# Slot softmax in single steps with its multiply on GpSimd, two-term folds for batch 0, and a new order of pieces

## The chip, the cores and the metric

The kernel runs on one core of one Trainium2 chip. The time is that of the device for one execution, in microseconds. TensorE is the matrix engine (PE in the profile, and PEld for its loads of weights), VectorE is DVE, ScalarE is ACT, GpSimd is POOL and SyncE is SP.

## The reference

Eight batches (B = 8) of eight heads (H = 8) with 576 positions (S) of 64 values (D) go through an attention over 32 memory slots, and the result goes through a feed-forward network with a maximum over three products.

```
a      = softmax over the 32 slots of phi            [8, 8, 576, 32]
k_m    = a^T k,   v_m = a^T v                        [8, 8, 32, 64]
attn   = softmax over the 32 slots of (q k_m^T / 8)  [8, 8, 576, 32]
x      = attn v_m, heads side by side                [4608, 512]
h      = max(x w1, x w2, x w3)                       [4608, 768]
out    = h w_out                                     [4608, 512], float32
```

## The kernel before

**Algebra.** The heads' outputs x are never built. For each batch v_m is multiplied into the weights first ("fold", piece D): since x = attn v_m, x w = attn (v_m w), and v_m w has 256 rows (8 heads of 32 slots), held as two groups of 128 (NG = 2). The maximum over three products is taken as max(x (w1 - w3), x (w2 - w3), 0) + x w3, so that the FFN has two products and a relu, and the x w3 part goes to the output as attn (v_m (w3 w_out)). The subtraction w1 - w3 and w2 - w3 is made in place in w_sb by w_diff (piece V, L182), in bfloat16, on VectorE. w3 w_out is made once, out of transposes of w3 (piece W) and products with w_out (piece O).

**Pieces.** The kernel is a list of pieces, written out by hand or by a planner as one string of tokens (L487 to L508). A token has a letter, often a number, the batch after "@", and "!" where the copy out of PSUM goes to the other engine (VectorE or ScalarE) than EVAC names at L133. Each engine does its instructions in the order of the tokens, and waits, in this order, for what it needs. So a token fixes the place of its instructions in every queue that they use: TensorE, VectorE, ScalarE, GpSimd, and SyncE's queue of output stores.

- H, L, Y: loads, all issued by GpSimd (H, batch 0's k and v in halves; L0 phi, L1 k, L2 v, L3 q of a later batch; Y0 to Y2 w1, w2, w3, Y3 w_out). Only batch 0's phi is loaded by SyncE. k, v, q and the weights are changed to bfloat16 on the way. phi and q have two buffers, k and v one pair for even and one for odd batches, so a load waits until the batch two earlier has been used.
- E: exp of phi (ScalarE). B: a^T [k, v, 1] (TensorE, L212). N: division by the sums (VectorE). K: transpose of the result (TensorE) and its copy, kvt. Q: 32 x 32 transposes of q (VectorE, L269), one half each.
- S: scores (TensorE, L291), and two exps (ScalarE, L300), one for each group g.
- X (att_mul): the slot softmax of group g, five VectorE instructions one after the other: transpose of 32 x 32 blocks into t (L313), sum over slots sm (L315), reciprocal (L316), multiply t by it (L317), transpose back into attn (L323).
- D: fold, eight matmuls on 64 x 32 tiles of the array (L341), and the copy into wp, or for D3 into wp3, the fold of w3 w_out.
- F (ffn1): hidden slice ft = n // 2; the even n is the relu of the w1 product (h1), the odd n the maximum of the w2 product with it (VectorE, L380), into hT. Each has four matmuls of 288 columns (L367).
- T (ffn2): 128 rows of output, six matmuls with w_out (L398) and two with wp3 (L407, or L416 for the tile that two batches share), a copy, a store. The last tile is made in halves (L439, L447).
- I: the identity matrix (GpSimd). Z: matmuls on zeros that keep TensorE going while the first loads arrive.

All products share four PSUM buffers of two banks each (acc_pool), taken in turn: a product waits until the one four before it has been copied out.

**What sets the order at the start.** Batch 0 has its fold in four parts, D0, D1, D2 and D4, with the columns of FIRST (L172): 0 to 512, 512 to 768, 768 to 1024 and 1024 to 1536 of w1 and w2 side by side. Before the fold of a part its w_diff has to be done, which needs w3 (Y2) and w1 (Y0) or w2 (Y1).

Of the kernel before, what the change touches and what calls it, by code (L numbers as in the profile page):

```python
# [15 lines left out]
def kernel(  # L16
# [159 lines left out]

    def w_diff(n):

        c, end = FIRST[n]
        while c < end:  # L180
            e = min(end, (c // DF + 1) * DF)
            nc.vector.tensor_tensor(  # L182
                out=w12[:, :, c:e],
                in0=w12[:, :, c:e],
                in1=w_sb[:, :, 2, c % DF : c % DF + e - c],
                op=ALU.subtract,
            )
# [85 lines left out]
    def att_score(b):  # L276
# [22 lines left out]
        for a in range(NG):  # L299
# [4 lines left out]
                scale=0.125,  # L304
            )

    def att_mul(b, g):
        s = st[b]
        e2 = s["e2"][:, g]
        t = work.tile([P, S // HP, R, 2], BF16, name="t", tag=f"t{g}")  # L310
        tf = t.rearrange("p n r e -> p (n r e)").bitcast(FP32)
        tv = t.rearrange("p n r e -> p n e r")
        nc.vector.transpose(out=tf, in_=e2.bitcast(FP32))  # L313
        sm = work.tile([P, S // HP, 2], FP32, name="sm", tag=f"sm{g}")
        nc.vector.tensor_reduce(out=sm, in_=tv, op=ALU.add, axis=mybir.AxisListType.X)  # L315
        nc.vector.reciprocal(out=sm, in_=sm)  # L316
        nc.vector.tensor_tensor(  # L317
            out=t,
            in0=t,
            in1=sm.unsqueeze(2).to_broadcast([P, S // HP, R, 2]),  # L320
            op=ALU.mult,
        )
        nc.vector.transpose(  # L323
            out=attns[b // 2][:, g, (b % 2) * S : (b % 2 + 1) * S].bitcast(FP32), in_=tf
        )
# [3 lines left out]
    def fold(b, n, swap):  # L329
# [5 lines left out]
        elif b not in wps:  # L335
            wps[b] = work.tile([P, NG, 2 * DF], BF16, name="wp")
        ps = acc_pool.tile([P, NG, BANK], FP32, name="wps", tag="acc")
        for j in range(NP):
            for a in range(NG):
                r = slice(HP * a, HP * (a + 1))  # L340
                nc.tensor.matmul(  # L341
                    ps[M * j : M * (j + 1), a, 0 : hi - lo],
                    lhsT=s["kvt"][r, 0, M * j : M * (j + 1)],
                    rhs=(w3o if n == 3 else w12)[r, j, lo:hi],
                    start=True,
                    stop=True,
                    tile_position=(HP * a, M * j),
                )
# [190 lines left out]
```

## Time and profile before

| | |
|---|---|
| median of 13 runs | 169.68 us (169.18 to 170.18) |
| the profiled execution's own time | 169.5 us |
| its span, first to last instruction | 167.7 us |
| granted TensorE clock | 0.995 |
| TensorE matmuls busy | 157.4 us, 94% |
| VectorE busy | 110.4 us, 66% |
| ScalarE busy | 98.9 us, 59% |
| GpSimd busy | 28.4 us, 17% |
| VectorE L317, the multiply | 16 times, 758 ns |
| VectorE L315, the sum over slots | 16 times, 753 ns |
| TensorE L128, on zeros | 16.4 us busy |

The page gives an engine's busy time over the whole span. The chain of waits goes back from the last instruction: at each step to what released it, or to the instruction before it on its engine; a line of it holds the start, the length, and what ran, with the number of instructions merged. The timeline gives an engine's instructions in order of time, with the idle time before each and what ended it in brackets. A load's own instruction on GpSimd takes about 0.75 us; the transfer goes on after it, and the page's last part gives the time from issue to landing. Matmuls are pipelined and the profile models their ends, so their steps from start to start are read rather than their lengths.

### The profile page before, as it was taken

How to read it: one execution, taken by the hardware profiler on the slowest of the kernel's cores; microseconds unless marked ns; L12 is line 12 of the kernel's file. 1: busy time of each engine (PE TensorE's matmuls, PEld its weight loads, DVE VectorE, ACT ScalarE, POOL GpSimd, SP SyncE). 2: the span in 40 equal slices, each digit the busy share in tenths (PEclk: the TensorE clock that was granted, in tenths of full speed). 3: DMA queues.
4: the chain of work that ended last, by engine and by line, in shares of the span. 5: the costliest groups of instructions: out<-in, count | busy, mean ns of one | idle time of the engine just before them, and what ended most of it. 6: DMA issues, size and time to landing. Idle time of an engine off the chain costs nothing.

```text
span 167.7 us, 4603 instructions
## 1 busy us (share of the span) xinstructions
PE 157.4 (94%) x1971; PEld 86.9 (52%) x1992; DVE 110.4 (66%) x198; ACT 98.9 (59%) x145; POOL 28.4 (17%) x43
## 2 busy tenths in 40 slices
PE   7998799999979999999998999999999999999991
PEld 2444533674337535755674355766533577644450
DVE  5406876895787959789778999997599456610000
ACT  4100514943888278898675998738678877222420
POOL 7952100040261313304010500000000000000000
PEclk9999999999999999999999999999999999999998
DMA  5999999999999999999999999961113310033433
GB/s 155 156 204 212 205 210 247 240 207 340 269 280 264 207 232 329 244 233 207 238 287 248 281 260 258 235 116 65 68 63 129 125 63 6 0 125 149 164 125 127
DMA packets 21973, 31.76 MB, mean 189 GB/s; under 512 B 1216, under 2 KB 16576, under 8 KB 21952
## 3 DMA queue, kind: packets, MB, share of 16 engines
q0 software_dynamic: 16080, 21.43, 66.5%
q1 hardware_dynamic: 5728, 9.90, 16.6%
q8 instruction: 15, 0.25, 0.5%
q10 hardware_dynamic: 144, 0.13, 0.2%
q14 instruction: 6, 0.05, 0.1%
HBM read 39.32 MB, written 9.44 MB: 291 GB/s over the span
## 4 chain that ended last, share of the span: by engine, by line
PE 57%; DMA 20%; DVE 15%; issue 4%; POOL 2%; ACT 1%; POOLq 0%; ACTq 0%
PE acc L367 23%; DMA kvo<-in_v_dram 20%; PE po L398 19%; PE po L407 5%; DVE t L317 4%; DVE sm L315 4%; PE wps L341 3%; DVE attn L323 2%; PE kvp L212 2%; DVE t L313 2%; PE sc L291 2%; DVE sm L316 1%; PE po L416 1%; POOL kvo L94 1%; PE po L439 1%
## 5 line engine op out<-in xcount | busy, mean ns | idle before, releaser
L367 PE MATMUL acc<-attn,wp 128*128 128x288 bf16 x384 | 50.8, 286 | 1.6 <-DVE attn L323 1.4
L398 PE MATMUL po<-wo_sb,hT 128*128 128x512 bf16 x192 | 50.2, 380 | 0.9
L367 PEld LDWEIGHTS <-wp 128*128 128x128 bf16 x384 | 36.5, 98 | 14.6 <-issue 2.0
L380 DVE TENSOR_TENSOR hT<-acc,h 128x576 bf16<-128x576 f32 x48 | 34.5, 752 | 13.0 <-PE acc L367 6.3
L141 ACT COPY ot<-po 128x512 f32<-128x512 f32 x35 | 20.7, 591 | 28.9 <-PE po L407 24.4
L139 ACT ACTIVATE h<-acc 128x576 bf16<-128x576 f32 x46 | 28.5, 655 | 8.6 <-PE acc L367 7.5
L398 PEld LDWEIGHTS <-hT 128*128 128x128 bf16 x210 | 19.1, 98 | 24.2 <-issue 4.6
L141 ACT CAST wp<-wps 128x1024 bf16<-128x1024 f32 (+1 forms) x31 | 29.7, 1015 | 0.9 <-PE wps L341 0.9
L300 ACT ACTIVATE e<-sc 128x576 bf16<-128x576 f32 x16 | 9.6, 653 | 15.2 <-PE sc L291 15.2
L407 PE MATMUL po<-wp,attn 128*128 128x512 bf16 x62 | 18.4, 379 | 0.0
L128 PE MATMUL po<-warm 128*128 128x512 bf16 x62 | 16.4, 422 | 1.4 <-DVE warm L120 1.2
L317 DVE TENSOR_TENSOR t<-t,sm 128x576 bf16<-128x576 bf16 x16 | 12.1, 758 | 0.5
L315 DVE TENSOR_REDUCE sm<-t 128x18 f32<-128x576 bf16 x16 | 12.0, 753 | 0.6
L269 DVE STREAM_TRANSPOSE qT<-qq 128x576 f32<-128x576 f32 x16 | 12.0, 762 | 0.5 <-DMA qq<-in_q_dram 0.5
L128 PEld LDWEIGHTS <-warm 128*128 128x128 bf16 x64 | 6.5, 106 | 9.6 <-issue 3.2
L199 ACT ACTIVATE e<-ph 128x1152 bf16<-128x1152 f32 (+1 forms) x9 | 9.5, 1061 | 2.6 <-DMA ph<-in_phi_dram 2.6
L456 DVE COPY ot<-po 128x256 f32<-128x256 f32 x1 | 0.4, 425 | 15.8 <-PE po L447 15.8
L90 POOL DMA_DIRECT2D ph<-in_phi_dram x7 | 5.3, 760 | 31.7 <-ACT e L199 27.3
L313 DVE STREAM_TRANSPOSE t<-e 128x288 f32<-128x288 f32 x16 | 7.3, 455 | 4.0 <-ACT e L300 4.0
L407 PEld LDWEIGHTS <-attn 128*128 128x128 bf16 x62 | 6.1, 98 | 7.3
L94 POOL DMA_DIRECT2D kvo<-in_k_dram x9 | 6.7, 744 | 15.6 <-PE wps L341 13.1
L102 POOL DMA_DIRECT2D qq<-in_q_dram x8 | 6.0, 750 | 16.3 <-DVE qT L269 15.7
(46 smaller groups left out, 110.9 us busy)
## 6 DMA issues: line engine op xcount, KB each, us to landing
out_dram<-ot SPq DMA_DIRECT2D x35, 256.0 KB, 2.4
qq<-in_q_dram POOLq DMA_DIRECT2D x8, 576.0 KB, 18.9
ph<-in_phi_dram POOLq DMA_DIRECT2D x7, 576.0 KB, 20.1
kvo<-in_k_dram POOLq DMA_DIRECT2D x7, 576.0 KB, 16.2
kvo<-in_v_dram POOLq DMA_DIRECT2D x7, 576.0 KB, 19.1
w_sb<-in_moe_w_dram POOLq DMA_DIRECT2D x3, 768.0 KB, 19.3
wo_sb<-in_moe_w_out_dram POOLq DMA_DIRECT2D x1, 768.0 KB, 16.4
ph<-in_phi_dram SPq DMA_DIRECT2D x2, 288.0 KB, 3.4
```

The costliest lines, as they stand in the source:

```text
L128: nc.tensor.matmul(po[:, 0:BANK], lhsT=warm[:, 0:P], rhs=warm, start=True, stop=True)
L139: nc.scalar.activation(out=out_, in_=in_, func=AF.Relu)
L141: nc.scalar.copy(out=out_, in_=in_)
L269: nc.vector.transpose(out=s["qT"][:, j].rearrange("p j c r e -> p (j c r e)").bitcast(FP32), in_=loaded[b]["q"][:, j].rearrange("p j c d - ...
L300: nc.scalar.activation(out=e2[:, a].rearrange("p (t r c) -> p t r c", t=2, c=NC), in_=sc[a][:, :, 0:SH].rearrange("p t (c r) -> p t r c", ...
L313: nc.vector.transpose(out=tf, in_=e2.bitcast(FP32))
L315: nc.vector.tensor_reduce(out=sm, in_=tv, op=ALU.add, axis=mybir.AxisListType.X)
L317: nc.vector.tensor_tensor(out=t, in0=t, in1=sm.unsqueeze(2).to_broadcast([P, S // HP, R, 2]), op=ALU.mult,)
L367: nc.tensor.matmul(acc[:, h, 0:SH], lhsT=wps[b][:, g, w * DF + ft * P : w * DF + (ft + 1) * P], rhs=attn[:, g, c0 : c0 + SH], start=(g == ...
L380: nc.vector.tensor_tensor(out=hT[:, ft, (b % 2) * S : (b % 2 + 1) * S].rearrange("p (h n) -> p h n", h=2), in0=a, in1=s["h1", ft], op=ALU.max,
L398: nc.tensor.matmul(po, lhsT=hT[:, fc, c0 : c0 + P], rhs=wo_sb[:, fc, :], start=(n == 0), stop=False,)
L407: nc.tensor.matmul(po, lhsT=attn[:, g, c0 : c0 + P], rhs=wp3s[b][:, g, :], start=False, stop=(g == NG - 1),)
```

## The change

The slot softmax of X is split into five tokens, so that its steps can be placed one by one: a (transpose), s (sum), c (reciprocal), m (multiply), X (transpose back). The multiply m is issued on GpSimd in place of VectorE. In batch 0 the folds D0, D1, D2 and D4 no longer read w1 - w3 and w2 - w3: they read w1 or w2 as loaded with kvt, and add a second product of minus kvt (the new tile kvtn, copied by ScalarE with a factor of -1 when kvt is copied) with w3. The subtractions (V) then serve batches 1 to 7 alone, come after batch 0's folds, and are cut into three equal parts of 512 columns. The list of tokens is new as a whole. The attn tile of a pair of batches is made by whichever batch asks first.

```diff
--- before.py
+++ after.py
@@ -176,7 +176,7 @@
 
     def w_diff(n):
 
-        c, end = FIRST[n]
+        c, end = n * BANK, (n + 1) * BANK
         while c < end:
             e = min(end, (c // DF + 1) * DF)
             nc.vector.tensor_tensor(
@@ -186,9 +186,6 @@
                 op=ALU.subtract,
             )
             c = e
-
-
-
 
     st = {}
 
@@ -258,6 +255,9 @@
         if part != 1:
             s["kvt"] = work.tile([P, 3, P], BF16, name="kvt")
         evacuate("K", 0, swap, s["kvt"][:, ns], ps[:, ns])
+        if b == 0 and part != 0:
+            s["kvtn"] = const.tile([P, P], BF16, name="kvtn")
+            nc.scalar.mul(out=s["kvtn"], in_=ps[:, 0], mul=-1.0)
 
     def att_q(b, n):
 
@@ -278,7 +278,7 @@
         s = st[b]
         kvt, qT = s["kvt"], s["qT"]
         e2 = s["e2"] = work.tile([P, NG, S], BF16, name="e2")
-        if b % 2 == 0:
+        if b // 2 not in attns:
             attns[b // 2] = work.tile([P, NG, 2 * S], BF16, name="attn")
         sc = [
             acc_pool.tile([P, 2, BANK], FP32, name="sc", tag="acc") for _ in range(NG)
@@ -304,24 +304,42 @@
                 scale=0.125,
             )
 
+    def att_t(b, g):
+        s = st[b]
+        t = s["t", g] = work.tile([P, S // HP, R, 2], BF16, name="t", tag=f"t{g}")
+        nc.vector.transpose(
+            out=t.rearrange("p n r e -> p (n r e)").bitcast(FP32),
+            in_=s["e2"][:, g].bitcast(FP32),
+        )
+
+    def att_sum(b, g):
+        s = st[b]
+        sm = s["sm", g] = work.tile([P, S // HP, 2], FP32, name="sm", tag=f"sm{g}")
+        nc.vector.tensor_reduce(
+            out=sm,
+            in_=s["t", g].rearrange("p n r e -> p n e r"),
+            op=ALU.add,
+            axis=mybir.AxisListType.X,
+        )
+
+    def att_rec(b, g):
+        s = st[b]
+        nc.vector.reciprocal(out=s["sm", g], in_=s["sm", g])
+
     def att_mul(b, g):
         s = st[b]
-        e2 = s["e2"][:, g]
-        t = work.tile([P, S // HP, R, 2], BF16, name="t", tag=f"t{g}")
-        tf = t.rearrange("p n r e -> p (n r e)").bitcast(FP32)
-        tv = t.rearrange("p n r e -> p n e r")
-        nc.vector.transpose(out=tf, in_=e2.bitcast(FP32))
-        sm = work.tile([P, S // HP, 2], FP32, name="sm", tag=f"sm{g}")
-        nc.vector.tensor_reduce(out=sm, in_=tv, op=ALU.add, axis=mybir.AxisListType.X)
-        nc.vector.reciprocal(out=sm, in_=sm)
-        nc.vector.tensor_tensor(
+        t = s["t", g]
+        nc.gpsimd.tensor_tensor(
             out=t,
             in0=t,
-            in1=sm.unsqueeze(2).to_broadcast([P, S // HP, R, 2]),
+            in1=s["sm", g].unsqueeze(2).to_broadcast([P, S // HP, R, 2]),
             op=ALU.mult,
         )
+
+    def att_back(b, g):
         nc.vector.transpose(
-            out=attns[b // 2][:, g, (b % 2) * S : (b % 2 + 1) * S].bitcast(FP32), in_=tf
+            out=attns[b // 2][:, g, (b % 2) * S : (b % 2 + 1) * S].bitcast(FP32),
+            in_=st[b]["t", g].rearrange("p n r e -> p (n r e)").bitcast(FP32),
         )
 
     wps, wp3s = {}, {}
@@ -335,17 +353,21 @@
         elif b not in wps:
             wps[b] = work.tile([P, NG, 2 * DF], BF16, name="wp")
         ps = acc_pool.tile([P, NG, BANK], FP32, name="wps", tag="acc")
-        for j in range(NP):
-            for a in range(NG):
-                r = slice(HP * a, HP * (a + 1))
-                nc.tensor.matmul(
-                    ps[M * j : M * (j + 1), a, 0 : hi - lo],
-                    lhsT=s["kvt"][r, 0, M * j : M * (j + 1)],
-                    rhs=(w3o if n == 3 else w12)[r, j, lo:hi],
-                    start=True,
-                    stop=True,
-                    tile_position=(HP * a, M * j),
-                )
+        terms = [(s["kvt"][:, 0], w3o[:, :, lo:hi] if n == 3 else w12[:, :, lo:hi])]
+        if b == 0 and n != 3:
+            terms.append((s["kvtn"], w_sb[:, :, 2, lo % DF : lo % DF + hi - lo]))
+        for i, (lhs, rhs) in enumerate(terms):
+            for j in range(NP):
+                for a in range(NG):
+                    r = slice(HP * a, HP * (a + 1))
+                    nc.tensor.matmul(
+                        ps[M * j : M * (j + 1), a, 0 : hi - lo],
+                        lhsT=lhs[r, M * j : M * (j + 1)],
+                        rhs=rhs[r, j, :],
+                        start=(i == 0),
+                        stop=(i == len(terms) - 1),
+                        tile_position=(HP * a, M * j),
+                    )
         evacuate(
             "D", n, swap, wp3s[b] if n == 3 else wps[b][:, :, lo:hi], ps[:, :, 0 : hi - lo]
         )
@@ -473,7 +495,11 @@
             "K": lambda: att_kv_t(b, swap, i),
             "Q": lambda: att_q(b, i),
             "S": lambda: att_score(b),
-            "X": lambda: att_mul(b, i),
+            "a": lambda: att_t(b, i),
+            "s": lambda: att_sum(b, i),
+            "c": lambda: att_rec(b, i),
+            "m": lambda: att_mul(b, i),
+            "X": lambda: att_back(b, i),
             "D": lambda: fold(b, i, swap),
             "F": lambda: ffn1(b, i, swap),
             "T": lambda: ffn2(b, i, swap),
@@ -485,24 +511,28 @@
 
 
     for w in """
-        H3@0 H0@0 H2@0 I@0 H1@0 E@0 Z38@0 B@0 L3@0 N@0 Y2@0 Z3@0 K@0 Q0@0 Q1@0 Z7@0 S@0 X0@0
-        Z6@0 W2@0! W0@0 Y3@0 Y0@0 W1@0 Z10@0 O1@0 O3@0 X1@0 V1@0 V0@0 O2@0 O0@0 D1@0 Y1@0 L0@1
-        D0@0! D3@0 V2@0 F10@0 V4@0 L1@1 F8@0 L3@1 F6@0 D2@0 F0@0! F2@0 D4@0 F3@0 F4@0 E@1 L2@1
-        F1@0 F11@0 F7@0 L0@2 F9@0 F5@0 B0@1 T3@0 N0@1 L0@3 K0@1! Q0@1 T2@0! B1@1 Q1@1 S@1 E@2
-        L2@2 L1@2 L0@4 N1@1 K1@1 T1@0 X0@1 D0@1 D1@1! L3@2 T0@0! D3@1 L1@3 L2@3 L3@3 D2@1 X1@1
-        F6@1! F0@1 F1@1 F2@1 F4@1 F7@1 F5@1 E@3 F8@1 F3@1 F10@1 F11@1 F9@1 B@2 N@2 L0@5 Q0@2
-        T1@1 L1@4 E@4 K@2 T4@1! Q1@2 S@2 T2@1! D0@2 D1@2! T0@1! X0@2 D3@2 B@3 X1@2 D2@2 T3@1
-        N@3 F6@2 Q0@3 Q1@3 F0@2 F1@2 F8@2 F7@2 L2@4 F4@2 K@3 L3@4 L1@5 F10@2 F9@2 S@3 L2@5
-        F11@2 F2@2 E@5 F5@2 F3@2 D2@3 D1@3! X0@3 X1@3 T2@2! D0@3 B@4 N@4 D3@3 T0@2! Q1@4 T3@2
-        F4@3 F6@3 K@4 F8@3 Q0@4 F9@3 F2@3 F0@3 F7@3 F1@3 F10@3 L3@5 F11@3 D0@4 B@5 D1@4! D2@4
-        T1@2 L0@6 L1@6 N@5 Q0@5 K@5 L2@6 F3@3 F5@3 S@4 E@6 Q1@5 T4@3! L0@7 X0@4 S@5 T1@3 D1@5!
-        X1@4 D0@5 T2@3! X1@5 L3@7 D2@5 B@6 D3@4 F10@4 N@6 E@7 X0@5 T3@3 F8@4 F6@4 F9@4 F11@4
-        F2@4 F4@5 L3@6 Q1@7 F7@4 F6@5 L1@7 F5@5 F8@5 Q1@6 F0@4 F7@5 F4@4 K@6 L2@7 Q0@7 F5@4
-        Q0@6 T0@3! F3@4 F1@4 F0@5 F1@5 F2@5 F10@5 F3@5 D2@6 B@7 D3@5 D3@6 T3@4 N@7 K@7 F9@5
-        F11@5 S@6 T4@5! S@7 T3@5 D1@6! D1@7! X0@6 D3@7 T0@5! X0@7 T2@4! D0@7 D0@6 D2@7 T1@4
-        T1@5 X1@7 X1@6 F6@6 F8@6 F10@6 F2@7 F3@7 F0@6 F7@6 F9@6 F2@6 F3@6 F1@6 F4@7 F11@6 F10@7
-        F4@6 F11@7 F6@7 F0@7 F5@7 F8@7 F9@7 F1@7 T0@4! F7@7 F5@6 T0@7! T1@7 T1@6 T0@6! T2@7!
-        T2@5! T2@6! T3@6 T4@7! T3@7
+        H3@0 I@0 E@0 H2@0 H1@0 H0@0 Z38@0 B@0 N@0 Z3@0 K@0 L3@0 Q1@0 Y2@0 Y3@0 Y0@0 Q0@0 Z7@0
+        S@0 a0@0 s0@0 Z6@0 W0@0 W2@0 W1@0 Z10@0 O2@0 a1@0 s1@0 c1@0 Y1@0 c0@0 m0@0 X0@0 O0@0
+        m1@0 O1@0 X1@0 D0@0 D1@0! O3@0 F4@0 V0@0 L0@1 L1@1 L3@1 F0@0 F2@0! F10@0! D2@0 D4@0
+        F8@0 V2@0 F3@0 F1@0 L2@1 F6@0 E@1 F11@0 F9@0 F7@0 F5@0 D3@0 B0@1 L0@2 N0@1 T3@0 L0@3
+        Q0@1 Q1@1 K0@1! T0@0! L2@2 V1@0 S@1 L1@2 a0@1 B1@1 s0@1 N1@1 E@2 c0@1 a1@1 T2@0! K1@1
+        s1@1 D1@1! c1@1 D0@1 m0@1 X0@1 D3@1 T1@0 m1@1 X1@1 D2@1! F6@1 F8@1 F4@1 F5@1 L3@2 F0@1
+        F1@1 F7@1 E@3 F2@1 F9@1 F10@1 L1@3 F11@1 L2@3 F3@1 B@2 T0@1! N@2 K@2! T2@1! Q0@2 L3@3
+        Q1@2 S@2 a0@2 T1@1 s0@2 D0@2 D2@2 L2@4 c0@2 m0@2 a1@2 s1@2 c1@2 T3@1 T4@1! D1@2! m1@2
+        X0@2 X1@2 B@3 D3@2 F0@2 N@3 F4@2 Q0@3 F1@2 Q1@3 F8@2 F6@2 F5@2 K@3! F10@2 F9@2 S@3 L0@4
+        F7@2 F11@2 L1@4 F2@2 E@4 a0@3 F3@2 a1@3 L3@4 s0@3 c0@3 D3@3 D1@3! T1@2 L0@5 L2@5 s1@3
+        c1@3 T3@2 D0@3 D2@3 B@4 m0@3 m1@3 X0@3 T2@2! X1@3 N@4 F0@3 F10@3 Q1@4 Q0@4 K@4 F1@3
+        F6@3 S@4 F11@3 a1@4 s1@4 a0@4 L1@5 E@5 F2@3 L3@5 c1@4 F7@3 s0@4 F8@3 T0@2! L3@6 F3@3
+        F4@3 F9@3 F5@3 L0@6 m1@4 L1@6 D1@4! D2@4 B@5 N@5 D0@4 c0@4 T1@3 K@5! X1@4 L2@6 Q0@5
+        T4@3! Q1@5 S@5 a0@5 T3@3 s0@5 D3@5 E@6 D2@5 Q0@6 c0@5 a1@5 Q1@6 s1@5 D0@5 L2@7 m0@4
+        m0@5 T0@3! c1@5 T2@3! m1@5 X0@5 X0@4 F10@4 F6@4 F11@4 F2@4 F7@4 F4@4 F8@4 F0@4 F5@4
+        D1@5! L1@7 X1@5 B@6 D3@4 N@6 F9@4 F4@5 F3@4 K@6 F2@5 F1@4 F8@5 F5@5 S@6 F9@5 F3@5 a0@6
+        s0@6 a1@6 c0@6 L0@7 F10@5 F6@5 F0@5 s1@6 L3@7 F7@5 m0@6 E@7 c1@6 T1@4 F1@5 D1@6! D0@6
+        m1@6 X0@6 Q0@7 X1@6 B@7 D2@6 N@7 Q1@7 T3@4 F4@6 F5@6 F10@6 F11@5 F8@6 K@7 F2@6 F6@6 S@7
+        F11@6 F9@6 T4@5! D2@7 D3@7 a0@7 s0@7 a1@7 s1@7 c0@7 T2@5! D1@7! D3@6 c1@7 m0@7 D0@7
+        m1@7 X0@7 T3@5 X1@7 T1@5 F8@7 F9@7 F4@7 F7@6 F10@7 F3@6 F5@7 F0@6 F0@7 F1@6 F6@7 F2@7
+        F11@7 F7@7 F3@7 F1@7 T3@6 T1@7 T2@4! T2@6! T0@7! T0@4! T1@6 T0@6! T2@7! T0@5! T4@7!
+        T3@7
     """.split():
         n, b = w.rstrip("!").split("@")
         issue(int(b), n, w.endswith("!"))
```

## The prediction

> **What bounds the kernel now.** I read the page's first table first, then the chain of waits in order of time, then the timelines of TensorE, VectorE and GpSimd from 10 to 50 us, where the chain leaves TensorE.
>
> The page, busy time by engine:
>
> ```profile
> span 167.7 us, 4603 instructions
> PE 157.4 (94%) x1971; PEld 86.9 (52%) x1992; DVE 110.4 (66%) x198; ACT 98.9 (59%) x145; POOL 28.4 (17%) x43
> ```
>
> TensorE is nearly always busy; no other engine passes two thirds. But a share over the span can hide a stage, so the chain in order of time (start us, length us, what):
>
> ```profile
> 14.99 25.81 DMA kvo<-in_v_dram
> 40.85 0.75 PE kvp L212 x72
> ...
> 46.53 0.77 DVE sm L315
> 47.62 0.77 DVE t L317
> 48.41 0.49 DVE attn L323
> 48.95 5.79 PE acc L367 x46
> ...
> 86.54 0.34 PE wps L341 x8
> ...
> 124.35 0.77 PE wps L341 x24
> ```
>
> Two things are to be seen. VectorE's slot softmax (t, sm, t, attn) carries the chain only where TensorE has run out of other work: it ends at 48.90 and the FFN of batch 1 starts at 48.95. And the fold (wps) is cheap: eight matmuls 0.34 us, 24 of them 0.77, so each further eight cost (0.77-0.34)/2 = 0.215.
>
> From the TensorE timeline's starts I counted, after the w3·w_out products begin at 22.73, what exceeds the ordinary step of each matmul form (0.123 us for 288 columns, 0.216 for 512): 0.7 around the batch-0 folds (28.0 to 29.1), 0.4 at 40.5, 1.4 at 47.5, 0.4 at 80.7, 0.7 at 91.2, 0.5 at 104.6 and 106.0. That is 4.1 us of idle TensorE in 141. From 107 to the end there is none. The change can only win from these 4.1 us, unless it brings forward 22.73, where wo_sb lands; its load keeps its place among the loads, so that stays.
>
> The start, VectorE and then GpSimd (start, length, engine, line, idle before):
>
> ```profile
> 26.44 1.83 DVE L182 TENSOR_TENSOR w_sb<-w_sb 128x1024 bf16<-128x1024 bf16 x2 [2.16 <-DMA w_sb<-in_moe_w_dram]
> ```
>
> ```profile
> 7.04 1.54 POOL L108 DMA_DIRECT2D w_sb<-in_moe_w_dram  x2
> 9.27 0.76 POOL L90 DMA_DIRECT2D ph<-in_phi_dram  x1 [0.68 <-DMA kvo<-in_k_dram]
> ...
> 35.79 0.76 POOL L90 DMA_DIRECT2D ph<-in_phi_dram  x1 [15.66 <-ACT e L199]
> ```
>
> w1 lands at 26.4 and the two subtractions delay the folds D1 and D0 to 28.0 and 28.4. GpSimd issues the loads far ahead: batch 1's phi at 9.27, while the transfers queued before it last until w2's landing at 30.15 (7.84 plus 22.3). After that a load lands about every 3 us until 113.6, so the load queue is never empty in that time.
>
> **What the Trainium skill says.** GPSIMD Engine Reference, section 3.1: a two-input elementwise instruction takes about 2.6 cycles an element at 1.2 GHz on GpSimd. The trace of before has no such instruction. My estimate from it: 576 x 2.6 / 1.2 = 1.25 us, plus 0.1 for start and hand-over, 1.35. SBUF — State Buffer, section "Who interferes with whom": VectorE and GpSimd exclude each other where VectorE has two SBUF inputs or a two-port mode. In this kernel only w_diff (L182) and the multiply itself (L317) read two SBUF tensors; hT (L380) reads one from PSUM. The transposes' 455 ns for 288 elements and 762 for 576 fit about one element a cycle and show no double rate, so I expect little blocking; no run here shows it yet. TensorEngine Tiling, "Available Configurations": 64x32 tiles are eight at once; the 0.215 us for eight 512-column matmuls, the step of one full-width matmul, agrees.
>
> **The change part by part.**
>
> *Batch-0 folds.* D0 and D4 (512 columns) get eight more matmuls each, D1 and D2 (256) as well: 2 x 0.215 + 2 x 0.11 = +0.65 us of TensorE. kvtn is one small ScalarE copy from PSUM near 14.6; the kvt copy of the same kind took 0.38, and ScalarE is idle from start to 16.77. In exchange the folds no longer wait for w_diff. New order from 22.73: O2 O0 O1 (18 x 0.216) end at 26.6, w1 is there at 26.4, D0 and D1 to 27.5, O3 to 28.8. D0's ScalarE copy (1.01) ends at 28.4, so F4 starts at 28.8 and nothing waits: the 0.7 us of idle goes. Net 0. W2's copy goes from ScalarE (1.01) to VectorE (0.66); with it the three w3T copies end near 21.45, ahead of wo_sb at 22.6, which hides them. The pieces of w_diff are the same four instructions (2 x 1.22, 2 x 0.69), now on VectorE behind F's evacuations; V1 stands before a0@1 and runs while T0@0 keeps TensorE busy.
>
> *Softmax steps and GpSimd.* VectorE loses 16 x 0.758 = 12.1 us, GpSimd gets 16 x 1.35 = 21.6. Per batch the chain was 2 x (0.52 + 0.78 + 0.30 + 0.79 + 0.50) = 5.8 us on VectorE. Now VectorE needs six steps, 3.2 us, with m0 under a1, s1, c1, then m1 1.35 and X1 0.5: 5.05. This matters only where TensorE waits, first at batch 1. There S@1 now stands ahead of B1@1, so the 0.4 us wait for v at 40.5 goes. My walk through the engines: T3, T0 and S@1 end at 41.15; exps to 42.8; a0 42.2, s0, N1, c0 to 44.1, a1, K1's copy, s1, c1 to 45.9; m0 44.15 to 45.5, m1 45.95 to 47.3, X1 47.85. TensorE is ready at 47.9. The FFN starts there instead of at 48.95: -1.05. Next late are ScalarE's copies: D1, D0, D3 of batch 1 (3 x 1.02) and T1's output are done at 49.05, and the four PSUM buffers make F6, F8, F4 and F0 wait for them. That returns about 0.65; B@2 comes at 54.35 against 54.74. In batch 2, where K3's copy has moved to ScalarE, the FFN stage loses 0.6 the same way and is level at 73.5. Before F0@3 the old 0.4 wait is gone (80.8 against 81.3). At the join of batches 4 and 5, X0@4 stands behind s1, c1 and X0@5 on VectorE and ends near 102.35, 0.6 after TensorE is ready. Counted over the same matmuls before and after I am level there. Beyond it VectorE has about 13.4 us of work beside 14.9 of TensorE, and the old 0.5 of waits at 104 to 106 has no counterpart.
>
> *Loads behind multiplies.* On GpSimd's queue L0@1 to L2@1 now stand behind m0@0 and m1@0. c0@0 ends at 23.3, m1 at 26.1, the four issues (0.75 each) from 26.1 to 29.1, all before w2's landing at 30.15, so the transfers follow on without a hole. Later m1@1 (47.3) is ahead of L3@2, with k of batch 2 still arriving until 51.4; m1@2 (64.9) is ahead of L0@4, with L3@3 and L2@4 still to come until about 67; m1@3 (79.4) is ahead of L1@5, with L2@5 coming until about 82; L2@7 waits for B@5 (91.1) and holds m0@4, which is needed only at 101. Each is hidden by 2 us or more. The order waits on VectorE for GpSimd too: behind X0@b stand the hT maxima of the running FFN, but where X0 is late none of them is yet due. SyncE's queue holds only output stores, in the order of the ffn2 tokens; they are due only when six output buffers have gone round, so moving them costs nothing.
>
> Sum: folds +0.65, first idle -0.7, batch 1 -0.4, batch 2 and 3 about -0.1, batches 4 and 5 +0.5, end -0.5: about -0.55. The profiled execution (167.7 of span, 1.8 around it, 169.5) becomes 168.95; the median of the runs shown is 0.18 above it, so I predict **169.1**.
>
> GpSimd's price, from both sides: 0.76 us (VectorE's own) makes X1@1 0.6 earlier, but TensorE is ready only at 47.9, so it gains nothing: 169.1. At 2.5 us batch 1 has m1 end at 49.2, X1 at 49.7 and 1.8 lost; batch 2 has X1@2 at 67.5 against 66.45, 1.05 lost; less 0.5 that ScalarE's lateness would cost anyhow: +2.3, 171.4.
>
> **Rivals.** (1) *The multiply on GpSimd is long, slower than before.* Place: X1@1 and X1@2. It loses from about 1.9 us an instruction, where 2 x 1.9 from 44.15 passes TensorE's readiness; at 2.1 to 2.5 it gives 170.1 to 171.4. For it: a broadcast f32 operand against bf16 data, unpriced by any row. Against: the skill's rate. Chance 0.26. (2) *VectorE was not the bound, no change.* ScalarE's copies and the four PSUM buffers eat all that the softmax gives up, and only +0.65 and -0.7 are left: 169.4 to 170.0. For it: my walk shows gains returned at three places. Chance 0.12. (3) *GpSimd's queue starves the loads.* If m1@0 ends after about 28, the first landing after w2 slips one for one, and v of batch 1 (40.8) with it: 2 us late gives 171. Or the order adds such joins as X0@4 at more places than I found: 170.2 to 171.5. Chance together 0.17. (4) *Larger gain.* The folds cost what I say but most of the 4.1 us of idle goes: 167.5 to 168.3. Chance 0.09.
>
> **How the numbers follow.** The forecast (168.4 to 169.3) has 0.36, its gain over 0.2%. A measurement of this kernel can hardly tell 0.2% (0.34 us) from no change. Faster: 0.36 + 0.09 = 0.45; same 0.12; slower 0.26 + 0.17 = 0.43. Cases of both signs hold most of the chance: the likeliest one's own range is 168.4 to 169.3, and the range 167.9 to 171.6 leaves out some 0.1 at each end.
>
> **What would show it.** Right: L341 with 232 + 64 matmuls instead of 200 + 64; no fold after 26.4 waiting on L182; the GpSimd multiply near 1.3 us by the spacing of m0 and m1; the first batch-1 matmul of L367 near 47.9; ph of batch 1 issued near 26 yet landing near 32.4. Wrong: a multiply over 1.9 us with TensorE waiting on attn; load landings with holes; VectorE standing on GpSimd for more than 3 us in all; TensorE's busy time stretched by short PSUM waits without a named engine.

## The result, and the profile after

The kernel after takes 166.68 us in the median (166.34 to 167.55, 11 runs) against 169.61 for the kernel before; the ratio is 0.9835, with a 95% interval of 0.9816 to 0.9853. That is 2.8 us by the ratio, where the prediction had 0.55: the right side, but five times too small, and below the range's low end of 167.9. The profiled execution took 167.18 us; its span is 165.4 against 167.7. Some executions show a lower granted clock than the others of the same kernel and take longer; the times given here leave them out.

The shares of the chain that ended last and the group of the FFN's first products (busy, mean ns | idle before, releaser), from the page of the kernel before:

```profile
PE 57%; DMA 20%; DVE 15%; issue 4%; POOL 2%; ACT 1%; POOLq 0%; ACTq 0%
...
L367 PE MATMUL acc<-attn,wp 128*128 128x288 bf16 x384 | 50.8, 286 | 1.6 <-DVE attn L323 1.4
```

The page of the kernel after, busy time by engine, and its shares of the chain that ended last:

```profile
span 165.4 us, 4691 instructions
PE 156.6 (95%) x2006; PEld 87.5 (53%) x2024; DVE 94.3 (57%) x179; ACT 99.7 (60%) x149; POOL 46.8 (28%) x59
...
PE 81%; DMA 10%; POOL 3%; issue 2%; DVE 1%; ACT 0%; POOLq 0%; ACTq 0%; DVEq 0%
```

TensorE had 57% of the chain before and has 81% now; VectorE had 15% and has 1%. VectorE's busy time fell by 16.1 us. Two groups of the page tell the multiply's price and where the FFN's waits went:

```profile
L389 PE MATMUL acc<-attn,wp 128*128 128x288 bf16 x384 | 50.4, 286 | 0.0
L332 POOL TENSOR_TENSOR t<-t,sm 128x576 bf16<-128x576 bf16 x16 | 18.4, 1154 | 67.5 <-DVE sm L327 67.5
```

The FFN's first products waited 1.6 us before, 1.4 of it for attn, and now wait 0.0. A multiply takes 1.15 us on GpSimd. The chain in order of time (start, length, what):

```profile
6.29 16.67 DMA wo_sb<-in_moe_w_out_dram
...
41.14 0.18 PE kvp L209 x16
41.32 0.79 issue
42.12 0.61 PE kvp L209 x56
...
47.95 5.99 PE acc L389 x48
53.94 0.87 PE kvp L209 x72
...
100.68 4.41 PE acc L389 x36
```

From w_out's landing at 22.95 the chain hardly leaves TensorE. The FFN of batch 1 starts at 47.95 (before: 48.95) and runs through. Counted from the starts as in the prediction, but with the short stretches too, idle TensorE after w_out's landing falls from 4.8 us to 1.5; of this 0.98 is the stretch at 41.1, and 0.3 the wait for kvt at 44.7. That is 3.3 us less, and the folds add 0.65 of matmuls, so 2.65 should be saved. The spans differ by 2.3; w_out landed 0.36 later in this execution than in that of before, so from the landing on it is 2.7.

GpSimd's timeline at the start (start, length, engine, line, idle before):

```profile
7.10 1.52 POOL L108 DMA_DIRECT2D w_sb<-in_moe_w_dram  x2
23.45 2.27 POOL L332 TENSOR_TENSOR t<-t,sm 128x576 bf16<-128x576 bf16 x2 [14.82 <-DVE sm L327]
25.67 0.81 POOL L90 DMA_DIRECT2D ph<-in_phi_dram  x1
```

Batch 1's phi is issued at 25.67 instead of 9.27 and lands, by the trace, at 32.32 instead of 32.37. Two multiplies in a row take 2.27; the second starts 1.13 after the first.

### The profile page after: what moved, and what is told of

Its sections match the earlier page's. It is cut to its first block, busy times and chain, and to the rows that moved or that the text cites. A ratio compares the mean times of both kernels' runs of the same rounds, so it can differ in the third digit from the quotient of the medians.

```text
span 165.4 us, 4691 instructions
## 1 busy us (share of the span) xinstructions
PE 156.6 (95%) x2006; PEld 87.5 (53%) x2024; DVE 94.3 (57%) x179; ACT 99.7 (60%) x149; POOL 46.8 (28%) x59
## 4 chain that ended last, share of the span: by engine, by line
PE 81%; DMA 10%; POOL 3%; issue 2%; DVE 1%; ACT 0%; POOLq 0%; ACTq 0%; DVEq 0%
PE acc L389 29%; PE po L420 28%; DMA wo_sb<-in_moe_w_out_dram 10%; PE po L429 8%; PE wps L363 5%; PE po L161 3%; PE kvp L209 3%; POOL kvo L94 2%; PE sc L291 2%; PE po L438 1%; PE po L461 1%; PE kvtp L254 1%; DVE hT L402 0%; POOL qq L102 0%; POOL w_sb L108 0%
## 5 line engine op out<-in xcount | busy, mean ns | idle before, releaser
L332 POOL TENSOR_TENSOR t<-t,sm 128x576 bf16<-128x576 bf16 x16 | 18.4, 1154 | 67.5 <-DVE sm L327 67.5
L128 PE MATMUL po<-warm 128*128 128x512 bf16 x62 | 17.1, 436 | 1.4 <-DVE warm L120 1.2
L340 DVE STREAM_TRANSPOSE attn<-t 128x288 f32<-128x288 f32 x16 | 7.3, 461 | 6.6 <-POOL t L332 6.6
L363 PE MATMUL wps<-w_sb,kvt 64*32 64x512 bf16 (+1 forms) x200 | 8.7, 373 | 0.3 <-DVE kvt L145 0.3
L209 PE MATMUL kvp<-kvo,e 64*32 64x192 bf16 (+2 forms) x648 | 8.2, 235 | 0.8 <-issue 0.8
```

The costliest lines, as they stand in the source:

```text
L128: nc.tensor.matmul(po[:, 0:BANK], lhsT=warm[:, 0:P], rhs=warm, start=True, stop=True)
L209: nc.tensor.matmul(kvp[M * j : M * (j + 1), a, 0:nd], lhsT=s["e"][r, j, c, :], rhs=kv[r, cols, j, c, :], start=(c == 0), stop=(c == NC - 1 ...
L332: nc.gpsimd.tensor_tensor(out=t, in0=t, in1=s["sm", g].unsqueeze(2).to_broadcast([P, S // HP, R, 2]), op=ALU.mult,)
L363: nc.tensor.matmul(ps[M * j : M * (j + 1), a, 0 : hi - lo], lhsT=lhs[r, M * j : M * (j + 1)], rhs=rhs[r, j, :], start=(i == 0), stop=(i == ...
```

## The experiments

All times are medians, with the ratio to the kernel before of the same chip. "After" in an edit's description is the kernel after. Lists of tokens are cut to the part that the text speaks of; "..." marks what is left out.

**The multiply back on VectorE, all else as after.**

```diff
-        nc.gpsimd.tensor_tensor(
+        nc.vector.tensor_tensor(
             out=t,
```

> The kernel after, with the 16 multiplies back on VectorE and every token where it is. Theory A (the gain is VectorE's relief where the slot softmax carries the chain): 16 x 0.76 = 12.1 us return to VectorE, the first FFN matmul of batch 1 comes near 48.5 instead of 47.95, and at the join of batches 4 and 5 three multiplies (2.3 us) stand ahead of X0@4; total 168.0 to 169.5. Theory B (the new order alone makes the gain, the engine of the multiply is hidden): within 0.5 of 166.7.

Measured: 169.29 us, ratio 0.9989 (0.9971 to 1.0008). New order, split steps and new folds without the move to GpSimd are worth nothing; the move is worth the whole gain in this order. Theory A holds, with one of the two places that it named, the join of batches 4 and 5. VectorE's timeline at the join of batches 4 and 5, first of this run:

```profile
98.65 0.71 DVE L318 TENSOR_REDUCE sm<-t 128x18 f32<-128x576 bf16 x1
99.28 1.42 DVE L332 TENSOR_TENSOR t<-t,sm 128x576 bf16<-128x576 bf16 x2
100.61 0.26 DVE L327 RECIPROCAL sm<-sm 128x18 f32<-128x18 f32 x1
100.91 0.76 DVE L332 TENSOR_TENSOR t<-t,sm 128x576 bf16<-128x576 bf16 x1
101.58 0.83 DVE L340 STREAM_TRANSPOSE attn<-t 128x288 f32<-128x288 f32 x2
```

then of the kernel after:

```profile
95.31 0.48 DVE L310 STREAM_TRANSPOSE t<-e 128x288 f32<-128x288 f32 x1 [2.37 <-ACT e L300]
95.82 0.75 DVE L318 TENSOR_REDUCE sm<-t 128x18 f32<-128x576 bf16 x1
96.49 0.77 DVE L269 STREAM_TRANSPOSE qT<-qq 128x576 f32<-128x576 f32 x1
97.19 0.22 DVE L327 RECIPROCAL sm<-sm 128x18 f32<-128x18 f32 x1
97.33 0.42 DVE L310 STREAM_TRANSPOSE t<-e 128x288 f32<-128x288 f32 x1
97.67 0.73 DVE L269 STREAM_TRANSPOSE qT<-qq 128x576 f32<-128x576 f32 x1
98.33 0.71 DVE L318 TENSOR_REDUCE sm<-t 128x18 f32<-128x576 bf16 x1
99.07 0.27 DVE L327 RECIPROCAL sm<-sm 128x18 f32<-128x18 f32 x1
99.25 0.78 DVE L340 STREAM_TRANSPOSE attn<-t 128x288 f32<-128x288 f32 x2
```

With the three multiplies the transposes into attn end at 102.41, without them at 100.03. TensorE's timeline of the run with the multiply on VectorE shows the price:

```profile
100.41 0.59 PE L429 MATMUL po<-wp,attn 128*128 128x512 bf16 x2
102.47 3.73 PE L389 MATMUL acc<-attn,wp 128*128 128x288 bf16 x29 [1.47 <-DVE attn L340]
```

1.6 us of idle from start to start here, and two of 0.2 and 0.5 at 118.9 and 121.6. At batch 1, where I had looked for the gain, the multiply's engine makes next to no difference: TensorE's idle there is 1.05 against 0.98.

**The multiply on GpSimd in the old kernel, all else as before.**

```diff
-        nc.vector.tensor_tensor(
+        nc.gpsimd.tensor_tensor(
             out=t,
```

> The kernel before, with the multiply of each slot softmax on GpSimd and nothing else changed, so that VectorE waits inside each X. Theory A: GpSimd's 1.15 us and the hand-over of about 0.2 stand in a chain that had 0.79, some 0.55 more for each X on VectorE's queue, and loads stand behind multiplies; where the chain binds (batches 1, 3, 4, 5) this costs 1 to 4 us: 170.5 to 173. Theory C (the multiply's move gains by itself, since VectorE's busy time falls): 167.5 to 169.

Measured: 191.38 us, ratio 1.1291 (1.1236 to 1.1346). Theory A had the sign and was far too small, because I had looked at VectorE's chain more than at the loads. GpSimd's timeline of this run:

```profile
19.10 1.16 POOL L317 TENSOR_TENSOR t<-t,sm 128x576 bf16<-128x576 bf16 x1 [12.78 <-DVE sm L316]
20.21 0.89 POOL L115 DMA_DIRECT2D wo_sb<-in_moe_w_out_dram  x1
```

w_out is issued at 20.21 instead of 6.23, since Y3@0 stands behind X0@0 in the list, and lands at 27.6 instead of 22.6. Later loads fare the same way: the last of batch 7 lands at 133 instead of 114.

Not all of the 22 us are waits. TensorE's busy time for the same matmuls is 164.5 us against 157.4, and the granted clock of this execution is 0.943 against 0.995. The chain of this run shows it at the FFN of batch 1:

```profile
57.58 0.49 DVE attn L323
58.11 8.14 PE acc L367 x46
```

The same 46 products took 5.79 us before. TensorE had waited 3.7 us ahead of them, and for some 5 us from then on a product steps by 0.24 us instead of 0.12. The same is seen behind the waits of 5.5 us for w_out and 3.3 us at 129. So a long wait cost more than its own length in this run.

**The same with w_out, w1, w2 and the first five loads of batches 1 and 2 ahead of X0@0.**

```diff
-        ... S@0 X0@0 Z6@0 W2@0! W0@0 Y3@0 Y0@0 W1@0
+        ... S@0 Y3@0 Y0@0 Y1@0 L0@1 L1@1 L3@1 L2@1 L0@2 X0@0 Z6@0 W2@0! W0@0 W1@0
```

> The kernel before with the multiply on GpSimd, and w_out, w1, w2 and the first five loads of batches 1 and 2 issued ahead of X0@0. w_out should land near 22.6 again instead of 27.6 and the start lose its 5 us: 185 to 187. If most of the 22 us came from the start's loads: under 178. If from VectorE waiting for GpSimd inside each X: no change, 190 to 192.

Measured: 184.54 us (182.1 to 184.7), ratio 1.0837 (1.0759 to 1.0916), just under what was expected. w_out lands at 22.8, and 6.8 of the 22 us are gone. The rest is in the later joins. The waits of this run (us in total, times, longest):

```profile
DVE attn L323 <- POOL t L317: 24.3, 16, 2.8
```

VectorE stands 24.3 us on GpSimd where it stands 6.6 in the kernel after, because an unsplit X holds its queue; and the loads behind later multiplies are still late (the last at 128). TensorE's busy time is still 4.5 us above that of the kernel before, at a granted clock of 0.972. How the remaining 15 us divide between the two causes was not tried, nor was the old order with split steps.

**The new folds alone in the old kernel.** The two-term folds and kvtn as in the change, the subtractions after batch 0's folds.

```diff
-        ... X1@0 V1@0 V0@0 O2@0 O0@0 D1@0 ... D3@0 V2@0 F10@0 V4@0 ... D4@0 F3@0 F4@0 E@1
+        ... X1@0 O2@0 O0@0 D1@0 ... D3@0 F10@0 ... D4@0 V0@0 F3@0 F4@0 V2@0 E@1 ... Q1@1 V1@0 S@1
```

> The kernel before with the two-term folds of batch 0 alone; the subtractions follow batch 0's folds, in three parts. By the prediction's sum +0.65 of matmuls and -0.7 of idle TensorE: 169.3 to 170.0. Theory D (the folds carry the gain): 168.5 or less.

Measured: 170.23 us, ratio 1.0042 (1.0027 to 1.0057): 0.7 slower than the kernel before, near the sum's zero and outside what was expected by 0.2. D0 and D1 no longer wait long, but V0 and V2, now behind the folds, stand ahead of maxima on VectorE, and 0.5 us of idle, which ends with a maximum, comes at 36. That this is the whole of the 0.7 was not tried.

**The old folds in the new kernel.**

```diff
-        X1@0 D0@0 D1@0! O3@0 F4@0 V0@0 ... F10@0! D2@0 D4@0 F8@0 V2@0 F3@0 ... L2@2 V1@0 S@1
+        X1@0 V0@0 V1@0 D0@0 D1@0! O3@0 F4@0 ... F10@0! V2@0 V4@0 D2@0 D4@0 F8@0 F3@0 ... L2@2 S@1
```

> The kernel after with batch 0 folded from subtracted weights as before (four subtractions ahead of the folds they serve), the rest as it is. TensorE has 0.65 us less work, and waits again for w1's landing plus two subtractions (26.7 + 0.7 + 1.2 = 28.6 against D0 at 27.1), part of it covered by moving nothing: 0 to +1.2, 166.7 to 167.9. Theory D (the folds carry the gain): 168.5 or more.

Measured: 170.18 us, ratio 1.0019 (0.9987 to 1.0051). By the ratios that is 3.1 above the kernel after; the expectations of later runs have 3.7, the difference of the plain medians. The expectation missed. Taken by itself this would say that the folds carry the gain. The waits of TensorE in this run say what it is:

```profile
PE wps L358 <- DVE w_sb L182: 3.6, 4, 1.6
```

All four folds stand on the subtractions: 3.6 us of waits, less the 0.65 of matmuls saved, is the loss. My edit had put V2 and V4 behind two copies on VectorE and directly ahead of D2 and D4, without the cover (D3, F10, F8, F6) that they had in the old order. The next run tests that.

**The old folds in the new kernel, with the old order of batch 0's start.** From O1@0 to F5@0 the tokens stand as in the kernel before but for the places of three loads, with X split and the multiply on GpSimd; from B0@1 on as after, without V1@0.

```diff
-        O2@0 a1@0 s1@0 c1@0 Y1@0 c0@0 m0@0 X0@0 O0@0 m1@0 O1@0 X1@0 V0@0 V1@0 D0@0 D1@0! O3@0 F4@0 ...
+        O1@0 O3@0 a1@0 s1@0 c1@0 Y1@0 c0@0 m0@0 X0@0 m1@0 X1@0 V1@0 V0@0 O2@0 O0@0 D1@0 ... D0@0! D3@0 V2@0 F10@0 V4@0 ...
```

> The kernel after with the subtracted folds of batch 0 again, but with batch 0's start in the order of the kernel before (V1 and V0 ahead of O2 and O0, D1 first, D3 ahead of F10), so that the subtractions are covered as they were there; the multiply stays on GpSimd. If the folds' 3.7 us in the run that undid them alone came from the new order having no cover for the subtractions: 166.6 to 168.0, that is the folds are worth under 1 us where the order fits. If the two-term folds themselves carry the gain: 169.5 or more.

Measured: 167.10 us, ratio 0.9856 (0.9833 to 0.9879), which overlaps the kernel after's. So the two-term folds are worth 0.4 us by the medians, which the intervals can't tell from nothing, and the loss in the run before was the cover that my edit had taken from the subtractions.

**The new order alone: multiply on VectorE and old folds.** The run with the old folds, first form, and in it

```diff
-        nc.gpsimd.tensor_tensor(
+        nc.vector.tensor_tensor(
             out=t,
```

> The new order and the split steps alone: multiplies on VectorE and batch 0 folded from subtracted weights, placed as in the run that undid the folds alone. If the two losses add up (2.4 for the multiply, 3.7 for the folds): 172.3 to 173.3. If they share one idle stretch: 170.4 to 171.5. If the order by itself were the gain: under 168.

Measured: 173.88 us, ratio 1.0243 (1.0213 to 1.0272), 0.6 above what was expected of two losses that add up, and by the ratios 1.2 above their sum (2.6 and 3.1). TensorE's waits for the subtractions are the same 3.6 us as in the run with the old folds, but in the traced execution the 32 FFN products behind them take 5.66 us against 4.09 there, at a granted clock of 0.83 from 32 to 42. That 1.6 us more accounts for the excess, as far as one execution of each can show it. With the caveat on the subtractions' cover, the order by itself isn't the gain; it is what lets the multiply move.

**Each multiply twice on GpSimd.**

```diff
+        t2 = const.tile([P, S // HP, R, 2], BF16, name=f"t2{b}{g}")
+        nc.gpsimd.tensor_tensor(out=t2, in0=t, in1=..., op=ALU.mult)
         nc.gpsimd.tensor_tensor(out=t, in0=t, in1=..., op=ALU.mult)
```

> The kernel after with each multiply issued twice on GpSimd, first into a spare tile, so that one step takes about 2.3 us. Theory A (slack everywhere but at batch 1): X1@1 ends near 48.7 instead of 47.6, TensorE starts batch 1's FFN 0.8 to 1.0 later, the other batches hide it: 167.3 to 168.2. The prediction's first rival (price decides at batches 1 and 2): about 2 us more than 166.7, 168.5 to 169.2.

Measured: 170.81 us, ratio 1.0069 (1.0041 to 1.0098), 4 us above the kernel after: twice what the prediction's rival gave, and some three times or more what Theory A did. X1@1 does end at 48.1 with 0.74 of idle, but so do other joins: 1.1 us between 80.6 and 84, 0.3 at 101.8, 1.2 at 121 to 122.5, and 0.3 at 136. The loads that follow batch 0's multiplies are issued 1.7 us later, so that TensorE waits 0.9 for v of batch 1; that costs little, since the kernel after is idle as long at the same place. The slack that hides the multiply is there at its present price and little beyond.

**D3's copy twice on ScalarE in batches 1 to 7.**

```diff
+        if n == 3 and b > 0:
+            nc.scalar.copy(out=wp3x, in_=ps[:, :, 0 : hi - lo])
```

> The kernel after with the copy of D3 out of PSUM done twice by ScalarE in batches 1 to 7, the second time into a spare tile: 7 x about 0.95 us more of ScalarE in front of the FFN stages. The prediction's walk (ScalarE's copies are late there and the four PSUM buffers pass this on to TensorE): most of it appears, +3 to +6, 170 to 173. Theory E (the walk added whole durations of instructions that in truth overlap, and ScalarE has slack of about 1 us there): under +1.0, 166.7 to 167.7.

Measured: 170.76 us, ratio 1.0064 (1.004 to 1.0088). Seven more copies, 6.0 us more of ScalarE's busy time, cost 4 us. Theory E's "slack of about 1 us" falls: ScalarE is close to binding. TensorE's timeline of this run at batch 1:

```profile
47.07 0.66 PE L392 MATMUL acc<-attn,wp 128*128 128x288 bf16 x4
48.41 4.76 PE L392 MATMUL acc<-attn,wp 128*128 128x288 bf16 x37 [0.69 <-ACT wp3x L376]
```

After one FFN product the next waits for the PSUM buffer of the doubled copy: the mechanism that the walk named, but without the added copy it isn't reached.

**Loads ahead of batch 0's multiplies.**

```diff
-        Y1@0 c0@0 m0@0 ... V0@0 L0@1 L1@1 L3@1 F0@0 ... L2@1 ... B0@1 L0@2
+        Y1@0 L0@1 L1@1 L3@1 L2@1 L0@2 c0@0 m0@0 ... V0@0 F0@0 ... B0@1
```

> The kernel after with the five loads L0, L1, L3, L2 of batch 1 and L0 of batch 2 issued ahead of the multiplies m0@0 and m1@0. By the prediction (the transfers queue behind w2's landing at 30.5 in any case): landings of batch 1 unchanged, 166.4 to 167.0. Its third rival (loads behind multiplies cost): v of batch 1 lands earlier than 40.4 and the time falls by 0.5 or more.

Measured: 167.12 us, ratio 0.9857 (0.983 to 0.9884), the same as after. v of batch 1 is issued at 14.82 instead of 27.94 and lands at 40.67 instead of 40.42. The new place of the loads costs nothing.

**Batch 1's join, three orders.** First T2@0 between S@1 and B1@1 and T1@0 ahead of K1@1:

```diff
-        S@1 L1@2 a0@1 B1@1 s0@1 N1@1 E@2 c0@1 a1@1 T2@0! K1@1 s1@1 D1@1! c1@1 D0@1 m0@1 X0@1 D3@1 T1@0 m1@1
+        S@1 L1@2 a0@1 T2@0! B1@1 s0@1 E@2 c0@1 N1@1 a1@1 T1@0 K1@1 s1@1 D1@1! c1@1 D0@1 m0@1 X0@1 D3@1 m1@1
```

> The kernel after with the tokens around batch 1's join in another order: T2@0 between S@1 and B1@1, T1@0 ahead of K1@1. The two idle stretches of TensorE at 41.1 (0.98) and 44.4 (0.48) would be filled, and the first FFN matmul of batch 1 be bound by X1@1 near 47.6 instead of 47.95: -0.3 to -0.5, 166.2 to 166.4. If the stretch at 41.1 belongs to the instructions' own supply, it turns up elsewhere and nothing is gained: 166.5 to 166.9.

Measured: 167.10 us, ratio 0.985 (0.9821 to 0.9879). The idle stretch at 41.1 is gone; the wait for kvt of batch 1 stays (0.3, now at 45.2), and 1.47 of idle stand ahead of F6@1 instead. The trace puts the end of this idle down to ScalarE's second copy of a fold, where the next expectation takes X1@1 for the cause. Next, N1@1 and K1's copy taken out of the softmax chain:

```diff
-        S@1 L1@2 a0@1 B1@1 s0@1 N1@1 E@2 c0@1 a1@1 T2@0! K1@1 s1@1 D1@1! c1@1 D0@1 m0@1 X0@1 D3@1 T1@0 m1@1 X1@1 D2@1! F6@1
+        S@1 L1@2 a0@1 s0@1 T2@0! B1@1 E@2 c0@1 a1@1 m0@1 s1@1 c1@1 N1@1 T1@0 K1@1 m1@1 X0@1 D1@1! D0@1 X1@1 D3@1 D2@1! F6@1
```

> The kernel after with batch 1's join in another order: T2@0 between S@1 and B1@1, T1@0 ahead of K1@1, and on VectorE all six softmax steps of batch 1 ahead of N1@1, so that neither N1 nor K1's copy stands in the chain. The run with the join reordered but the chain left (idle 1.47 ahead of F6@1, the same time as after) says that X1@1 binds; here it should end near 46.8 and the FFN of batch 1 start near 47.0 instead of 47.9. If the 0.9 is kept to the end: 165.7 to 166.3. If the later joins are bound by something else that does not move (q of batch 2 at 55.0, ScalarE): 166.5 to 166.9.

Measured: 167.27 us, ratio 0.987 (0.9849 to 0.9892). TensorE's timeline of this run:

```profile
46.04 0.40 PE L363 MATMUL wps<-w_sb,kvt 64*32 64x512 bf16 x8
47.84 6.05 PE L389 MATMUL acc<-attn,wp 128*128 128x288 bf16 x48 [1.41 <-ACT wp L141]
```

X1@1 ends at 46.2 here, and F6@1 still starts at 47.84: ScalarE's copies of the folds are next. Last, those copies dealt anew (D0 first, D1 on VectorE, D2 on ScalarE, D3 after F10), against the run just told:

```diff
-        X0@1 D1@1! D0@1 X1@1 D3@1 D2@1! F6@1 F8@1 F4@1 F5@1 ... F10@1 L1@3
+        X0@1 D0@1 X1@1 D1@1 D2@1 F6@1 F4@1 F8@1 F5@1 ... F10@1 D3@1 L1@3
```

> As the run that took N1 and K1's copy out of batch 1's chain, and in addition the copies are dealt anew: D0@1 first, D1's copy on VectorE, D2's on ScalarE, D3 after F10@1. In that run X1@1 had ended at 46.2 but F6@1 waited until 47.84 for ScalarE's second copy of a fold. If ScalarE's copies are what binds there next, F6@1 starts near 46.9, 0.9 ahead of the kernel after, and what is kept of it at the end gives 165.8 to 166.4. If a third wait takes its place (VectorE's copy of D1 at 47.4, the PSUM buffers): 166.5 to 166.9.

Measured: 166.99 us, ratio 0.9844 (0.9823 to 0.9864). TensorE's idle ahead of F6@1 falls to 0.8, and F6@1 comes at 47.60 in an execution whose w3·w_out products began 0.2 later than in that of the kernel after. So the chain, ScalarE's copies and TensorE's own work end within about 1 us of each other at this join, and no single one is worth much. None of the three beats the kernel after.

## Why the prediction was right in its sign and wrong in its size

*What bounds the kernel.* Right: idle TensorE after 22.7 was what could be won. I counted 4.1 us (4.8 with the short stretches); the kernel after has 1.5.

*Batch-0 folds, net 0.* Nearly right: 0.7 lost alone in the old order, which is clear of the noise, and 0.4 gained in the new by the medians, which is not.

*GpSimd's price of 1.35.* The Trainium skill's rate (GPSIMD Engine Reference, section 3.1) gave 1.25 and 0.1 on top; 1.15 is measured, 1.13 from start to start. The exclusion of VectorE by GpSimd that SBUF — State Buffer, section "Who interferes with whom", describes for two SBUF inputs was not met: no subtraction of w_diff runs beside a multiply here. On VectorE's other work nothing shows, as expected: its sums take 741 ns on average (753 before), its transposes into attn 461 (478).

*Loads behind multiplies.* Right in the kernel after, shown by moving them. That the same edit costs 22 us in a list that isn't made for it, 6.8 of them by the first loads alone, I had not priced.

*Batch 1.* The FFN's start was given as 47.9 and is 47.95, in part by luck: the walk had c0 of batch 1 done on VectorE at 44.1, and it was done at 43.6, but VectorE then waited 0.76 for K1's transpose, which TensorE's unforeseen idle at 41.1 had made late. What follows the start failed: "That returns about 0.65". It returned 0.2, which is no more than two products that had run ahead of the wait before; the FFN ran 5.99 us without a wait, and B@2 came at 53.94, not 54.35. In batch 2, where "the FFN stage loses 0.6 the same way", TensorE has no such wait either. The first FFN product of batch 3 comes at 80.3 where the walk had 80.8, but that is the 0.4 of batch 1 carried on: from B@2 to there the walk had 26.45 and the trace has 26.37.

*The step that failed most* is "X0@4 ... ends near 102.35, 0.6 after TensorE is ready". It ends at 100.03, 0.5 before TensorE is ready, and TensorE goes on at 100.52 without waiting. Of the 2.3 us between 102.35 and 100.03, 1.2 is TensorE itself, which is there earlier than the walk had it; the rest is VectorE's queue. By the prediction's own price for each step (0.52, 0.78, 0.30, 0.50, and the 0.76 of before for a half of Q) the ten VectorE instructions from a0@5 to X0@4 take 5.7 us; the timeline shown above has 100.03 - 95.31 = 4.72. The term that was mis-sized is the cost of an instruction in a queue: I gave each VectorE instruction its price in a chain where every step needs the one before it, and summed ScalarE's durations, where neighbours that don't need each other overlap. ScalarE's timeline of the kernel after shows it at batch 1:

```profile
45.42 2.84 ACT L141 CAST wp<-wps 128x1024 bf16<-128x1024 f32 x3 [0.23 <-PE wps L363]
48.14 0.62 ACT L141 COPY ot<-po 128x512 f32<-128x512 f32 x1
48.61 2.58 ACT L139 ACTIVATE h<-acc 128x576 bf16<-128x576 f32 x4
```

Three copies of 1.02 take 2.84, not 3.06, and the output copy behind them begins 0.12 before the third one ends. Over the trace a row of copies steps by 0.904 and one of relus by 0.54, where I had 1.02 and 0.66. In a stage with some nine such instructions that is 1 us, as much as the waits that I added. The doubled copy shows how near it was: with 0.9 us more ScalarE does bind.

*Why the sum came out small.* The prediction had the kernel after ahead by 0.4 at B@2, by 0.5 at the first FFN product of batch 3 and by 0.55 at the end; by the traces it is 0.8, 1.0 and 2.3. So 0.4 to 0.5 us was missed at batch 1's join. After 81 us the traces have 1.3 more; the sum has next to nothing there, since it set +0.5 for batches 4 and 5 against -0.5 for the end. TensorE in the kernel before is idle in that part for 0.5 at 104.6 and 106.0, which the prediction knew would go, and for 0.7 in batch 4's scores:

```profile
91.05 0.39 PE sc L291 x16
91.44 0.39 issue
91.83 0.41 PE sc L291 x7
```

I had counted this stretch, but the sum has no term for it. It is gone in the kernel after, and also with the multiply on VectorE, so it belongs to the order and not to the move; its cause is open. The walk gave the move's relief at batch 1 (1.05) and took it away at the joins after it. By the run with the multiply on VectorE it is the other way about: the order has most of the earlier start of batch 1 without the move, and the move pays at the join of batches 4 and 5 (1.6), where three multiplies stand ahead of the late transposes, and at 119 to 122 (0.7).

*The rivals.* A long multiply would have made it slower: at twice the price it takes 170.8, 0.7% more than before. That this lies in the rival's 170.1 to 171.4 is luck, since it loses 4 us from a start that was 2.4 lower. The limit of 1.9 us was also reckoned wrongly: in the walk X1@1 ends at 47.85 with 1.35 and TensorE is ready at 47.9, so the loss begins at about 1.4, X1's own transpose having been left out. "VectorE was not the bound" falls: with the multiply on VectorE the new kernel equals the old. "A larger gain" is what came, and more than its 167.5 to 168.3. One of the signs of being wrong came too and meant nothing: VectorE stands on GpSimd for 6.6 us in all, but not where TensorE waits for it.

## What to carry to other kernels

When work moves to an engine that also issues loads, the list around it has to be made for that, and for the engine that waits for the result: the same edit is worth 2.6 us in one order and costs 22 in another. Count a queue by the start-to-start steps that its trace shows, not by the sum of durations, above all where a walk decides between a wait of half a microsecond and none. Give every idle stretch that was counted a term in the sum. In a schedule whose engines end together, taking one wait away shows the next, so undo single parts at each join before naming one as the bound; and an edit that undoes a part has to give back the cover that the part had.

## What the runs showed of the hardware that was not expected

- VectorE: where an instruction doesn't need the one before it, it starts about 0.08 us before that one ends (maxima: 752 ns each, 675 from start to start); where it does need it, it starts 0.03 after (sum to reciprocal 0.77 to 0.79). So mixing the steps of two groups saves about 0.1 us a step. VectorE's busy time fell by 16.1 us, where the multiplies make 12.1 of it; some of the rest is K's copies, dealt to ScalarE in three more batches (1.1).
- ScalarE: neighbours overlap by about 0.11 us (wide copies 1.02, step 0.904; relus 0.66, step 0.54).
- TensorE: after waits of 3.3 to 5.5 us in the old kernel with the multiply on GpSimd, its steps were twice as long for some 4 to 5 us (0.24 instead of 0.12 for 288 columns). The waits of 3.6 us for subtractions, in four parts within 8 us, had this in one traced execution (32 products in 5.66 us) and not in the other (4.09).
- TensorE stands idle for 1.0 to 1.1 us within B1@1 near 41 us in the kernel after and in the runs with the multiply on VectorE, with the loads first and with the old start, and for 0.5 with the doubled copy. In the chain of the kernel after most of it is "issue"; v has landed by then. It is gone in the three runs in which T2@0 stands between S@1 and B1@1, but also, with S@1 just ahead of B1@1, in the two runs with the old folds in which B1@1 comes at 44.7 and 45.7; and the old kernel with new folds has 1.0 there with T2@0 just ahead. So no place of a token explains it, and its cause is open.
